# Expert weights loaded as one row and spread over the partitions by GpSimd, in place of transfers to 128 partitions

## The chip, the cores and the metric

The kernel runs on one core of one Trainium2 chip. The metric is the device time of one execution in microseconds; the time before is 358.34 us, the median of three runs (358.08 to 359.84).

## The reference

Two layers, one after the other. First attention with a learned block permutation: `sort_net` is normalised five times over rows and columns (Sinkhorn), the result mixes the 8 blocks of keys and of values of each of 4 batches x 8 heads, and softmax attention runs inside each block of 96 tokens. Its output, reshaped to 3072 tokens of 512 numbers, enters a mixture of four experts in which every token goes through every expert:

```
p = domain_probs / (domain_probs.sum(-1) + 1e-9)        # 3072 x 4
for e in range(4):
    h = maximum(x @ w1[e], 0)                            # 3072 x 1024
    out += p[:, e:e+1] * (h @ w2[e])                     # 3072 x 512
```

The change is about p, the expert weights of the tokens.

## The kernel before, in words

**Order.** The order of all instructions is written out by hand: each engine executes its own in program order, and an instruction waits by semaphore for what it reads or overwrites. Batch 0's attention runs first. From then on the experts' matmuls for 256 tokens at a time (a chunk; three chunks to a batch) alternate with pieces of the next batch's attention, which `PLANS` puts into numbered slots between the matmul groups.

**Where p is used.** In the hidden layer the tokens lie along the free axis and the features on the 128 partitions, so p of a token must stand on all partitions. The weight is put in where ReLU is applied, when a matmul result leaves PSUM: on VectorE in `chunk_first` (L821) and in `finish` (L1159), both `max(x, 0) * p`; on GpSimd in `finish2` (L1166), after a ReLU on ScalarE. So the tile `pb` (128 partitions x 4 experts x 256 tokens, float32) has to be there before the first eviction of a chunk.

**How pb is filled before.** `spread_weights` normalises p on VectorE and writes it to the scratch tensor `p_dram` (4 x 3072) in two transfers (L256, L258). `load_p` (L226 to 236) reads from it with a transfer whose source is repeated for 128 partitions; it is issued on SP, as are the attention's transposes (L413, L495), the copies of v (L405) and the stores. There is one `pb` buffer, so a load waits until the last eviction of the chunk before has read it. `load_p_one` (L238) does the same for one expert in a corner of the tile `Tt[3]`. `load_pair` (L1079) loads 256 tokens into `pb` and the next 256 into two half tiles. A chunk's load is issued by `chunk` (L845 to 851) behind the evictions of the chunk before it, with two transfers; in one chunk (batch 1, second) the second of these is held back until one product has been issued.

**GpSimd's work.** Its queue issues the loads of the expert weights `w1`, `w2` (L136 to 148, L1454 to 1479), of q, k, v (L107 to 126) and the accumulating transfers of `input_sums` (L1030). The transfers issued there use eight semaphores in turn, so the issue of one waits until the eighth before it has landed. Between them GpSimd executes `build_PI` for batch 1 (L360 to 377, four tensor_tensors), a few adds of results, and, in the last seven chunks, the multiplications of `finish2`.

**The last seven chunks** (from L1215 on). They use a scheme with seven products (Strassen-Winograd) for the first layer too. The first of them (`lead`) stands alone, the other six go in three pairs. VectorE makes the sums and differences of operands for it (`h_sums`, L779 to 791, with lines L785, L787, L789, L791 for the numbers 1 to 4; `pair_sums`, L1063; `input_sums`, L1027), all tensor_tensors with both inputs in SBUF. `load_pair` for the next pair is called in `last_second` (L1321) in the middle of the second layer of the chunk before it.

Of the kernel before, what the change touches and what calls it, by code (L numbers as in the profile page):

```python
# [2 lines left out]

# [15 lines left out]
def kernel(  # L19
# [11 lines left out]
    nc = tc.nc  # L31

    B, H, S, D = q.shape
# [4 lines left out]
    E = moe_w1.shape[0]  # L38
    FF = moe_w1.shape[2]
    P = 128  # L40
# [102 lines left out]
    def load_w2(e, parts=1):  # L143
        n = NFC // parts
        for i in range(parts):
            nc.gpsimd.dma_start(
                w2sb[e][:, ds(i * n, n)], moe_w2[e].rearrange("(fc p) d -> p fc d", p=P)[:, ds(i * n, n)]
            )
# [75 lines left out]
    pbs = {}  # L224

    def load_p(b, c, es=range(E), pb=None):  # L226
        if pb is None:
            pb = moe.tile([P, E, 2 * P], F32, name=f"pb_{b}_{c}", tag="pb", bufs=1)
        n = len(es)
        nc.sync.dma_start(  # L230
            pb[:, ds(es[0], n)],
            p_dram[ds(es[0], n), ds(b * S + 2 * c * P, 2 * P)].rearrange("(o e) x -> o e x", o=1).broadcast_to(
                [P, n, 2 * P]
            ),
        )
        return pb

    def load_p_one(b, c, e):  # L238

        pb = Tt[3].rearrange("p a f x -> p (a f x)")[:, 0:4 * P].bitcast(F32)  # L240
        nc.sync.dma_start(pb, p_dram[ds(e, 1), ds(b * S + 2 * c * P, 2 * P)].broadcast_to([P, 2 * P]))
        return pb

    def spread_weights():

        nc.vector.tensor_reduce(p_den, p_in, AX.X, ALU.add)
        yield
        nc.vector.tensor_scalar(out=p_den, in0=p_den, scalar1=1e-9, scalar2=None, op0=ALU.add)
        yield
        nc.vector.reciprocal(p_den, p_den)  # L250
        yield
        nc.vector.tensor_tensor(
            p_out.rearrange("p e t -> p t e"), p_in, p_den.broadcast_to([P, NT, E]), ALU.mult
        )
        p_rows = p_dram.rearrange("e (p t) -> p e t", t=NT)
        nc.sync.dma_start(p_rows[0:S_P], p_out[0:S_P])  # L256
        pbs[(0, 0)] = load_p(0, 0)
        nc.sync.dma_start(p_rows[S_P:P], p_out[S_P:P])  # L258
        yield

# [474 lines left out]
    def second_layer0(hf, slot):  # L735
        for t in range(R // 2):
            col = (R // 2) * hf + t
            po = psm([P, 2, 512], F32, f"ps_o_{col}")
            ps = po[:, 0, 0:Dm]
            for fc in range(NFC):  # L740
                nc.tensor.matmul(  # L741
                    ps, h0(fc)[:, ds(t * P, P)], w2sb[0][:, fc, :],
                    start=(fc == 0), stop=(fc == NFC - 1),
                )
                if fc == KH - 1:
                    slot()
            oaccs[col] = room[:, col - 2] if col > 1 else moeo.tile([P, Dm], F32, name=f"oacc_{col}", tag="oacc")
            nc.vector.tensor_scalar(
                out=oaccs[col][:], in0=ps, scalar1=p_sb[:, col], scalar2=None, op0=ALU.mult
            )  # L750
            slot()
# [82 lines left out]
    def chunk(b, c, slot, done=()):  # L834
# [8 lines left out]
            for e in es:  # L843
                h_sums(e, 2)
        nxt = (b, c + 1) if c + 1 < R // 2 else (b + 1, 0)  # L845
        first = int(nxt[0] == 0)
        pbs[nxt] = load_p(*nxt, range(first, first + 1))
        rest = lambda: load_p(*nxt, range(first + 1, E), pbs[nxt])
        late = b == c == 1
        if not late:  # L850
            rest()

        blk = lambda kh, tok: (lambda e, f: Hb[:, homes.get(e, e), kh * KH + f, ds(tok * P, P)])
        sm = lambda n: (lambda e, f: Sb[:, n, e, ds(f * P, P)])
# [26 lines left out]
        if b:  # L881
            times(bankA, blk(0, 0), "b11", es)
            slot()
            if late:
                rest()
            times(bankB, blk(1, 0), "b21", es)
            slot()
            nc.scalar.copy(p1[:], bankA)
            tt(oa1, bankB, p1[:], ALU.add)
            times(bankQ, sm(0), "t1", es)  # L890
            nc.scalar.copy(p5[:], bankQ)
            slot()
            for e in es:
                h_sums(e, 3, True)
            times(bankA, sm(1), "t2", es, False)
            nc.scalar.copy(u2[:], bankA)
            slot()
            for e in es:
                h_sums(e, 4, True)
            times(bankC, blk(1, 1), "n4", es)  # L900
            nc.scalar.copy(ob1, bankC)
            slot()
            times(bankA, blk(0, 1), "t3", es, False)
            tt(ob2, bankA, p5[:], ALU.add)
            slot()
            tt(ob1, bankA, ob1, ALU.add)
            store(1, ob)
            times(bankQ, blk(1, 0), "b22", es, False)
            tt(oa2, bankQ, u2[:], ALU.add)
            slot()  # L910
            store(0, oa)
            return
        if c:
            both = ob.rearrange("p (h d) -> p h d", h=2)
            times(bankA, blk(0, 0), "b11", es)
            slot()
            times(bankB, blk(1, 0), "b21", es)
            slot()
            tt(oa1, bankA, oa1, ALU.add)
            tt(oa1, bankB, oa1, ALU.add)  # L920
            if c == R // 2 - 1:
                h_sums(E - 3, 2)
            h_sums(E - 1, 2)
            times(bankC, blk(1, 1), "n4", es[:1], True, False)
            times(bankQ, sm(0), "t1", es)
            tt(ob2, bankQ, ob2, ALU.add)
            slot()
            for e in es:
                h_sums(e, 3)
            times(bankA, sm(1), "t2", es, False)  # L930
            tt(oa2, bankA, oa2, ALU.add)
            for e in es:
                h_sums(e, 4)
            slot()
            next(sums0)
            times(bankC, blk(1, 1), "n4", es[1:], False)
            tt(ob1, bankC, ob1, ALU.add)
            slot()
            times(bankA, sm(2), "t3", es, False)
            tt(both, bankA.rearrange("p (o d) -> p o d", o=1).broadcast_to([P, 2, DH]), both, ALU.add)  # L940
            slot()
            store(1, ob)
            next(sums0)
            times(bankQ, sm(3), "b22", es, False)
            tt(oa2, bankQ, oa2, ALU.add)
            slot()
            store(0, oa)
            return
# [6 lines left out]
        def f2():  # L955
            tt(oa1, product("p2", blk(1, 0), "b21"), oa1, ALU.add)
            slot()
# [22 lines left out]
            h_sums(e, 4)  # L980
        next(steps)
        f2()
        next(steps)
        h_sums(E - 1, 3)
        f3()
# [93 lines left out]
    def load_pair(g):  # L1079

        first, second = load_p(*divmod(g, R // 2)), []
        b, c = divmod(g + 1, R // 2)
        for n in range(2):
            t = att.tile([P, NB, 2, D], F16, name=f"pb7_{g}_{n}", tag="xsl").rearrange("p i h d -> p (i h d)")
            t = t.bitcast(F32).rearrange("p (e x) -> p e x", e=2)
            nc.sync.dma_start(
                t,
                p_dram[ds(2 * n, 2), ds(b * S + 2 * c * P, 2 * P)].rearrange("(o e) x -> o e x", o=1).broadcast_to(
                    [P, 2, 2 * P]
                ),  # L1090
            )
            second.append(t)
        pbs[g] = lambda j, e: first[:, ds(e, 1), :] if j == 0 else second[e // 2][:, ds(e % 2, 1), :]

    def last_banks(n):
# [373 lines left out]
            build_PI(nc.gpsimd, n, "k")  # L1469

    load_w2(1)
    load_w2(2)
    load_w1(3)
    def load_w2_part(e, d):
# [22 lines left out]
                f(*args)  # L1497

    second_layer0(0, next_stages)
    load_queries(1, range(2))  # L1500
    load_natural(1, "v", 0, 2, lambda: load_w2_part(3, DH))
    load_natural(1, "k", 0, 2)
    load_natural(1, "v", 1)
    load_natural(1, "k", 1)
    chunk_first(0, 0, [1, 2], 1, next_stages)
    pb_1 = load_p_one(0, 1, 1)
    h_sums(1, 4)
    for w in range(1, 5):
        h_sums(2, w)
# [3 lines left out]
    second_layer0(1, lambda: next(sums2, None))  # L1513
    sums0 = weight_sums(0, nc.vector)
    homes[1] = 0
    chunk_first(0, 1, [1], 1, next_stages, lambda e: pb_1.rearrange("p (o x) -> p o x", o=1))
    homes.clear()


    for g in range(G0 + 1):  # L1520
# [6 lines left out]
        def slot(b=b, c=c, at=at):  # L1527
            here = (c, at[0])
            for cc, n, f, *args in PLANS[b]:
                if (cc, n) == here:  # L1530
                    f(*args)
            if b:
                for cc, n, *args in PLAN_A:
                    if (cc, n) == here:
                        input_sums(*args)
                if here == (1, 12):
                    token_sums(G0, slice(0, 3))
                if here == (2, 0):
                    token_sums(G0, slice(3, 4))
            at[0] += 1  # L1540
# [6 lines left out]
    for g in range(G0 + 1, GN, 2):  # L1547
        last_second(g, last_first(g))
        last_second(g + 1, upper=True)
# [1 line left out]
_INS = ['q', 'k', 'v', 'sort_net', 'moe_domain_probs', 'moe_w1', 'moe_w2']  # L1551
_OUTS = [((3072, 512), 'float32')]
# [25 lines left out]
```

## Time and profile before

| what | us |
| --- | --- |
| median of 3 runs | 358.34 |
| the profiled execution, its own time | 358.21 |
| its span, first to last instruction | 356.3 |
| TensorE (PE) busy | 350.4 (98%) |
| VectorE (DVE) busy | 277.5 (78%) |
| ScalarE (ACT) busy | 170.1 (48%) |
| GpSimd (POOL) busy | 137.6 (39%) |
| transfers of `pb` and of the half tiles to 128 partitions | 20, of 128 to 512 KB each, landing 2.9 to 10.4 us after issue |
| the one transfer of `load_p_one` | 128 KB, landing after 12.6 |

The granted TensorE clock is full in every slice. The busy time of an engine says little by itself; the view of waits gives, for each engine, whom it waited for and how long, and the timeline gives its instructions in order with start, duration and the idle time before them. SPq and POOLq rows are the issues of transfers; a transfer lands later than its issue ends.

### The profile page before, as it was taken

The page shows a single profiled execution, that of the slowest core. Times are in us where ns is not written, and L with a number is a line of the kernel's source. Part 1 is how long each engine was busy: PE and PEld are TensorE (multiplying, and loading weights), DVE is VectorE, ACT ScalarE, POOL GpSimd, SP SyncE. Part 2 cuts the span into 40 slices and gives each one's busy share as a digit, 9 for nine tenths or more (in the row PEclk, how much of TensorE's full clock was granted, in tenths as well). Part 3 has the DMA queues.
Part 4 walks back from the last instruction along what each step waited for, and adds up shares of the span by engine and source line. Part 5 has one row for each costly group of instructions (what it writes and reads, how often), then busy time and mean ns, then how long its engine had stood idle before and what let it go on. Part 6 is the DMA issues. An engine that isn't in the chain of part 4 may idle for free.

```text
span 356.3 us, 9511 instructions
## 1 busy us (share of the span) xinstructions
PE 350.4 (98%) x3948; PEld 305.5 (86%) x3948; DVE 277.5 (78%) x555; ACT 170.1 (48%) x302; POOL 137.6 (39%) x154
## 2 busy tenths in 40 slices
PE   8899999999999999999999999999999999999996
PEld 8686857888888888988899888888888888888886
DVE  5766787779798687778879988896678886588963
ACT  2653330452425445368847259830288611598301
POOL 8766112466022420000626318840068800188400
PEclk9999999999999999999999999999999999999999
DMA  8999999999999999743995410005200014100021
GB/s 104 203 205 230 212 209 194 207 195 167 195 180 166 195 116 203 138 88 44 180 205 91 107 74 0 2 1 136 78 26 3 2 37 141 62 0 2 0 75 46
DMA packets 74762, 40.26 MB, mean 113 GB/s; under 512 B 41568, under 2 KB 70496, under 8 KB 74720
## 3 DMA queue, kind: packets, MB, share of 16 engines
q0 software_dynamic: 38720, 19.93, 43.2%
q1 hardware_dynamic: 35856, 19.67, 27.2%
q8 instruction: 31, 0.51, 0.6%
q14 instruction: 11, 0.09, 0.1%
q10 hardware_dynamic: 144, 0.07, 0.1%
HBM read 41.88 MB, written 6.34 MB: 135 GB/s over the span
## 4 chain that ended last, share of the span: by engine, by line
PE 95%; DVE 3%; issue 0%; DMA 0%; ACT 0%; DVEq 0%
PE ps_h L815 18%; PE ps_Q L1296 18%; PE ps_p L799 12%; PE ps_X L1153 10%; PE ps_Z L1153 7%; PE ps_Q L1153 7%; PE ps_Z L1296 6%; PE ps_h L704 3%; PE ps_o L741 3%; PE ps_p L860 3%; PE ps_a L479 2%; PE ps_s L444 2%; PE ps_k L425 1%; PE ps_v L391 1%; PE ps_mv L521 1%; PE ps_a L593 0%
## 5 line engine op out<-in xcount | busy, mean ns | idle before, releaser
L815 PE MATMUL ps_h<-xT,w 128*128 128x256 f16 x576 | 67.5, 273 | 0.0
L815 PEld LDWEIGHTS <-w 128*128 128x128 f16 x576 | 55.2, 98 | 7.3
L821 DVE SCALAR_TENSOR_TENSOR Hb<-ps_h,pb 128x1024 f16<-128x1024 f32 x34 | 41.5, 1223 | 17.8 <-PE ps_h L815 17.6
L1153 PEld LDWEIGHTS <-w 128*128 128x128 f16 x480 | 43.6, 98 | 4.7
L1166 POOL TENSOR_TENSOR arena<-tmp,pb 128x512 f16<-128x512 f32 x12 | 15.2, 1276 | 65.7 <-PE ps_Z L1153 49.8
L1296 PEld LDWEIGHTS <-Hb 128*128 128x128 f16 x320 | 31.1, 98 | 3.5
L1165 ACT ACTIVATE tmp<-tmp 128x512 f32<-128x512 f32 x46 | 29.0, 632 | 3.9 <-DVE tmp L1203 3.9
L1296 PEld LDWEIGHTS <-Sb 128*128 128x128 f16 x304 | 28.2, 98 | 3.0
L1153 PEld LDWEIGHTS <-arena 128*128 128x128 f16 x312 | 27.7, 98 | 2.8
L451 ACT ACTIVATE ET<-ps_s 96x768 f16<-96x768 f32 x24 | 18.1, 802 | 25.2 <-PE ps_s L444 25.0
L434 ACT CAST kT<-ps_k 64x384 f16<-64x384 f32 x48 | 22.7, 473 | 13.3 <-PE ps_k L425 12.3
L126 POOL DMA_DIRECT2D arena<-in_q_dram x24 | 19.9, 842 | 20.8 <-DMA q_ring<-arena 17.7
L1153 PE MATMUL ps_X<-ET,arena 128*128 128x256 f16 x168 | 25.2, 272 | 0.0
L1296 PE MATMUL ps_Q<-w,Hb 128*128 128x256 f16 x192 | 24.6, 273 | 0.0
L799 PEld LDWEIGHTS <-Hb 128*128 128x128 f16 x232 | 21.9, 98 | 3.0
L1159 DVE SCALAR_TENSOR_TENSOR Hb<-ps_X,pb 128x512 f16<-128x512 f32 x27 | 18.7, 692 | 7.0 <-PE ps_X L1153 7.0
L1173 ACT COPY ps_X<-ps_Z 128x512 f32<-128x512 f32 x27 | 15.4, 571 | 17.8 <-PE ps_Z L1153 17.8
L1153 PE MATMUL ps_Z<-xT,w 128*128 128x256 f16 (+1 forms) x176 | 22.5, 258 | 0.0
L785 DVE TENSOR_TENSOR Sb<-Hb 128x512 f16<-128x512 f16 x33 | 20.6, 646 | 0.0
L1180 ACT COPY tmp<-ps_X 128x512 f32<-128x512 f32 x26 | 15.2, 586 | 9.2 <-PE ps_X L1153 6.6
L1159 DVE SCALAR_TENSOR_TENSOR Hb<-ps_Z,pb 128x512 f16<-128x512 f32 x27 | 18.4, 683 | 1.3 <-PE ps_Z L1153 1.3
L1203 DVE TENSOR_TENSOR tmp<-ps_Q,tmp 128x512 f32<-128x512 f32 x26 | 17.7, 683 | 0.8 <-PE ps_Q L1153 0.8
(270 smaller groups left out, 744.3 us busy)
## 6 DMA issues: line engine op xcount, KB each, us to landing
w<-in_moe_w_dram POOLq DMA_DIRECT2D x4, 1024.0 KB, 27.2
w<-in_moe_w_dram POOLq DMA_DIRECT2D x6, 512.0 KB, 19.7
arena<-in_k_dram POOLq DMA_DIRECT2D x7, 384.0 KB, 7.6
arena<-in_v_dram POOLq DMA_DIRECT2D x7, 384.0 KB, 8.1
vs<-arena SPq DMA_DIRECT2D x36, 66.0 KB, 5.3
arena<-in_q_dram POOLq DMA_DIRECT2D x24, 96.0 KB, 7.5
out_dram<-ob SPq DMA_DIRECT2D x9, 256.0 KB, 2.0
pb<-p_dram SPq DMA_DIRECT2D x4, 512.0 KB, 5.8
```

The lines of the kernel that those rows point to most:

```text
L126: nc.gpsimd.dma_start(t[:, h // 2, :, h % 2, :], q[b, h].rearrange("(t p) d -> p t d", p=P))
L434: nc.scalar.copy(kT[ds(D * hh, D), r], pk[ds(D * r, D), hh].rearrange("p a (i c) -> p a i c", c=CP),)
L451: nc.scalar.activation(ETs[2 * (pr % 2) + hh][:, 0:S].rearrange("c (a x) -> c a x", a=2), pss[hh][0:BLK, :, 0:HS], AF.Exp, bias=0.0, scale ...
L785: tt(sm[0], blk(0, 1), blk(1, 1), ALU.add)
L799: nc.tensor.matmul(ps, lhs(e, f), Ts[e][rhs][:, f, :], start=(first and e == es[0] and f == 0), stop=(done and e == es[-1] and f == KH - 1 ...
L815: nc.tensor.matmul(ps[:, f, :], w1sb[e][:, kc, ds((4 * g + f) * P, P)], xT[:, kc, ds(2 * c * P, 2 * P)], start=(kc == 0), stop=(kc == NKC ...
L821: nc.vector.scalar_tensor_tensor(out=Hb[:, homes.get(e, e), ds(4 * g, 4), :], in0=ps[:], scalar=0.0, op0=ALU.max, in1=weights(e).broadcast ...
L1153: nc.tensor.matmul(dst[:, ds(f * cols, cols)], a[lhs][:, k, ds((f0 + f) * P, P)], t[rhs][:, k, :], start=(first and f == 0 and k == 0), st ...
L1159: nc.vector.scalar_tensor_tensor(out=home(i, j), in0=src.rearrange("p (f x) -> p f x", f=m), scalar=0.0, op0=ALU.max, in1=weight(j).broadc ...
L1165: nc.scalar.activation(src, src, AF.Relu, bias=0.0, scale=1.0)
L1203: tt(t12, Q, u2, ALU.add)
L1296: nc.tensor.matmul(ps, lhs(e, f), Ts[e][rhs][:, f, part], start=(first and e == 0 and f == 0), stop=(e == E - 1 and f == KH - 1), skip_gro ...
```

## The change

Each transfer to 128 partitions becomes a transfer to one partition (`load_rows`) and, at a place of its own further on in the program, a partition broadcast on GpSimd in place (`spread`): it reads the row in partition 0 and writes all 128 partitions. The two transfers of a chunk become one, of all its experts, and the one that was held back goes with it. The broadcast is an instruction of another GpSimd library, so a library is loaded once (between the issue of `w2` of experts 1 and 2), and the standard one again at the end. In the first chunk of all, expert 0's weights are no longer loaded; in the next one, expert 1's, which `load_p_one` brings. `load_p_one` is called before the loads of batch 1's q, k and v in place of behind the matmuls of the first chunk.

```
     def load_p(b, c, es=range(E), pb=None):
...
+        load_rows(pb[:, ds(es[0], len(es))], b, c, es)
+        return pb
+
+    def load_rows(dst, b, c, es):
         nc.sync.dma_start(
-            pb[:, ds(es[0], n)],
-            p_dram[...].rearrange("(o e) x -> o e x", o=1).broadcast_to([P, n, 2 * P]),
+            dst[0:1], p_dram[ds(es[0], len(es)), ds(b * S + 2 * c * P, 2 * P)].rearrange("(o e) x -> o e x", o=1)
         )
+
+    def spread(dst):
+        nc.gpsimd.partition_broadcast(dst, dst[0:1])
...
-        pbs[(0, 0)] = load_p(0, 0)
+        pbs[(0, 0)] = load_p(0, 0, range(1, E))
...
-        first = int(nxt[0] == 0)
-        pbs[nxt] = load_p(*nxt, range(first, first + 1))
-        rest = lambda: load_p(*nxt, range(first + 1, E), pbs[nxt])
-        late = b == c == 1
-        if not late:
-            rest()
+        first = 2 if nxt == (0, 1) else int(nxt[0] == 0)
+        pbs[nxt] = load_p(*nxt, range(first, E))
+        weights = pbs[nxt][:, first:E]
...
             times(bankA, blk(0, 0), "b11", es)          # chunk, batch 1
             slot()
-            if late:
-                rest()
+            spread(weights)
...
             times(bankB, blk(1, 0), "b21", es)          # chunk, batch 0, c > 0
             slot()
+            spread(weights)
...
         f2()                                            # chunk (0, 0)
+        spread(weights)
...
+            load_rows(t, b, c, range(2 * n, 2 * n + 2)) # load_pair
             second.append(t)
+        for t in (first, *second):
+            spread(t)
...
     load_w2(1)
+    nc.gpsimd.load_library(library_config.all_libraries[10])
+    spread(pbs[(0, 0)][:, 1:E])
     load_w2(2)
     load_w1(3)
...
     second_layer0(0, next_stages)
+    pb_1 = load_p_one(0, 1, 1)
     load_queries(1, range(2))
...
     chunk_first(0, 0, [1, 2], 1, next_stages)
-    pb_1 = load_p_one(0, 1, 1)
...
+    nc.gpsimd.load_library(library_config.standard)
```

More of the change, by code (lines that the diff above doesn't have):

```diff
@@ L5 @@
 import concourse.tile as tile
-from concourse import mybir
+from concourse import library_config, mybir
 from concourse.bass import ds
@@ L228, in load_p @@
             pb = moe.tile([P, E, 2 * P], F32, name=f"pb_{b}_{c}", tag="pb", bufs=1)
-        n = len(es)
+        load_rows(pb[:, ds(es[0], len(es))], b, c, es)
+        return pb
+    def load_rows(dst, b, c, es):
         nc.sync.dma_start(
-            pb[:, ds(es[0], n)],
-            p_dram[ds(es[0], n), ds(b * S + 2 * c * P, 2 * P)].rearrange("(o e) x -> o e x", o=1).broadcast_to(
-                [P, n, 2 * P]
-            ),
-        )
-        return pb
+            dst[0:1], p_dram[ds(es[0], len(es)), ds(b * S + 2 * c * P, 2 * P)].rearrange("(o e) x -> o e x", o=1)
+        )
+    def spread(dst):
+        nc.gpsimd.partition_broadcast(dst, dst[0:1])
     def load_p_one(b, c, e):
         pb = Tt[3].rearrange("p a f x -> p (a f x)")[:, 0:4 * P].bitcast(F32)
-        nc.sync.dma_start(pb, p_dram[ds(e, 1), ds(b * S + 2 * c * P, 2 * P)].broadcast_to([P, 2 * P]))
+        pb = pb.rearrange("p (o x) -> p o x", o=1)
+        load_rows(pb, b, c, [e])
+        spread(pb)
         return pb
@@ L1085, in load_pair @@
             t = t.bitcast(F32).rearrange("p (e x) -> p e x", e=2)
[L1086 to L1091, printed above, removed]
+            load_rows(t, b, c, range(2 * n, 2 * n + 2))
             second.append(t)
+        for t in (first, *second):
+            spread(t)
         pbs[g] = lambda j, e: first[:, ds(e, 1), :] if j == 0 else second[e // 2][:, ds(e % 2, 1), :]
@@ L1515 @@
     homes[1] = 0
-    chunk_first(0, 1, [1], 1, next_stages, lambda e: pb_1.rearrange("p (o x) -> p o x", o=1))
+    chunk_first(0, 1, [1], 1, next_stages, lambda e: pb_1)
     homes.clear()
```

## Prediction

> **What bounds the kernel.** I read the busy line of the page first, then the waits of TensorE, then the timelines of single engines where the change touches them.
>
> ```profile
> PE 350.4 (98%) x3948; PEld 305.5 (86%) x3948; DVE 277.5 (78%) x555; ACT 170.1 (48%) x302; POOL 137.6 (39%) x154
> ```
> ```profile
> PE ps_R L342 <- DVE sn L330: 1.2, 1, 1.2
> PE ps_w L276 <- DVE Hb L157: 1.1, 1, 1.1
> ```
>
> The two lines are the whole answer of the view of PE's waits (engine, tile and line, the releaser: total, times, longest). PE waits 2.3 us, both before 12 us, and then never again until its last matmul at about 353.4. The granted clock is full in all slices. So no wait on `pb` exists that could go away, and 512 KB less per chunk on the DMA engines shortens nothing: the change can only hide or add a stall. I therefore look for places where PE has little cover, and count everything against the profiled execution: 358.21 us, of which 356.3 are the span and 1.9 lie around it; the median of the runs shown, 358.34, is 0.1 above. Half a per cent is 1.8 us, and is about what a measurement of this kernel can tell from no change.
>
> The orders of PE, VectorE and ScalarE are the same in both kernels. On SP, 21 transfers to 128 partitions (20 and the one into `Tt[3]`) become 16 to one partition. GpSimd (POOL) has 18 instructions more: 16 broadcasts and two library loads.
>
> **Part 1: the library and the first broadcast.** The timeline of POOL's and SP's queues at that place (start, duration, line, what):
>
> ```profile
> 21.71 1.76 POOL L146 DMA_DIRECT2D w<-in_moe_w_dram  x2 [0.38 <-DMA w<-in_moe_w_dram]
> 23.50 0.75 POOL L139 DMA_DIRECT2D w<-in_moe_w_dram  x1
> 25.51 0.37 SPq L230 DMA_DIRECT2D pb<-p_dram  x1
> 26.10 0.89 POOL L1475 DMA_DIRECT2D w<-in_moe_w_dram  x1 [1.86 <-DMA w<-in_moe_w_dram]
> 27.00 1.06 POOL L372 TENSOR_TENSOR arena<-maskv,Rs 128x512 f16<-128x512 f16 x1
> ```
>
> The load of the library comes at 22.6, between the two issues of the first row. Its row of `p` is requested at 25.5 as before, and the broadcast waits for both. VectorE needs `pb` at 38.79 (L821), when the first matmul group of `chunk_first` ends; the group that reuses its PSUM buffer starts at 41.16, and the eviction takes 1.23, so PE is covered until the broadcast ends at 39.9. Behind it POOL has the loads of `w2` of expert 2, `w1` of 3, half of `w2` of 3, and the four `build_PI`. The transfers queued earlier hide these: `w2` of expert 1, issued at 21.71, lands 25.1 us later, at 46.8, and about 1 MB takes some 5 us of the 205 GB/s there, so the next one has to be in the queue by about 40. `build_PI` moves from 27 to 31 us to about 35 to 40, and is first read at 63.67 (L391).
>
> No row shows a library load or a broadcast. For the load the rows of the same congested stretch are: 1 us for a 16 KB block of code (the instruction queue: 31 packets, 0.51 MB, 0.6% of 16 engines' span) and 12.2 us for the slowest small transfer (L258, 36 KB). From 22.6 that ends between 23.6 and 34.8, and I take 10 us, towards the transfer, since it has to pass the same DMA engines. The row of 3 KB lies between 1.5 us (the 8 KB load of L77) and 10.4 (the whole 512 KB it replaces): 27 to 35.9. With 1.2 us for the broadcast the end lies at 28 to 37, ahead of 39.9: **0 us**. If the load took longer than 16 us, each further one would be PE's. [...] The second load, at the end, begins when POOL has finished, at 333.8; even 12.2 us end before 353: 0 us.
>
> **Part 2: the price of a broadcast.** It has one input and one output. The nearest rows are the COPY of 128x128 (L194, 0.29 us) and the adds L193 and L1166, 0.22 us at 16 elements and 1.27 at 512 (two inputs). A fixed 0.2 and 0.6 ns per element (COPY's 0.07 over 112 elements) is the lower end, 2.5 ns per element (L1166 whole) the upper. I take 0.2 us and 1.1 ns, towards COPY: 1.3 us for 1024 elements, 0.8 for 512, so 2.9 for the three of a pair (1.8 to 5.1).
>
> **Part 3: POOL's queue.** The row loads land at least as early as the transfers did, 1.5 to 8.6 us after the same SP places, and every broadcast ends before its first eviction. The one behind which most is queued is that of chunk (0, 2): POOL used to issue v and k of batch 2 at 79.84 and 80.57 and q from 81.30, but the row is requested at 85.22 only. With 2.5 to 4.5 us to land and 1.0 for the broadcast they move to about 90, q's first part to about 92. q lands up to 13.2 us after issue there, at 105, for the transpose that SP issued at 104.54, and PE uses its result at 114.23 (L444), 3.6 us behind the transpose's usual landing. Price 0. The first chunk's broadcast delays q by some 2 us at 65, with 3 us of cover (transposes at 76.82, their use at 86.15). The half that was held back at 172.26 now comes at 165.9 and delays one accumulating transfer by 1.3 us, which still lands some 5 us before its use. In all: **0 us**, up to 2.
>
> **Part 4: VectorE beside the broadcasts.** VectorE's sums read two operands from SBUF, and the profile shows what happens when GpSimd reads SBUF meanwhile:
>
> ```profile
> 196.41 1.28 POOL L1166 TENSOR_TENSOR Hb<-tmp7x,pb 128x512 f16<-128x512 f32 x1
> 196.69 1.28 DVE L785 TENSOR_TENSOR Sb<-Hb 128x512 f16<-128x512 f16 x1
> 197.64 1.45 POOL L1166 TENSOR_TENSOR Hb<-tmp7x,pb 128x512 f16<-128x512 f32 x1
> 197.89 1.48 DVE L785 TENSOR_TENSOR Sb<-Hb 128x512 f16<-128x512 f16 x1
> ```
>
> The add of L785 takes 0.42 alone (its median). Here each ends 0.28 us after the POOL instruction that had started before it: it waited for it to end. Two adds took 2.69 instead of 0.75, so of 2.68 us of POOL VectorE lost 1.94, about 0.7. [...]
>
> So I ask where VectorE's sums have less cover than 0.7 of the broadcasts beside them. At most sites it is over 1 us. In pairs two and three the rows are requested at 244.2 and 293.2; VectorE's sums of `pair_sums` end 2.9 us before PE reads them (251.98 against 254.87). The one place without cover is the load for the first pair, in the `lead` chunk:
>
> ```profile
> 200.30 1.42 DVE L787 TENSOR_TENSOR Sb<-Sb,Hb 128x512 f16<-128x512 f16 x4
> 201.64 1.42 DVE L791 TENSOR_TENSOR Hb<-Hb,Sb 128x512 f16<-128x512 f16 x4
> 202.98 1.43 DVE L789 TENSOR_TENSOR Hb<-Hb 128x512 f16<-128x512 f16 x4
> 204.92 0.42 DVE L1075 TENSOR_TENSOR kT<-xT 128x512 f16<-128x512 f16 x1
> ```
> ```profile
> 201.12 1.91 PE L1296 MATMUL ps_Q<-T,Sb 128*128 128x256 f16 x16
> 202.87 1.04 PE L1296 MATMUL ps_Q<-w,Hb 128*128 128x256 f16 x8
> 203.74 1.91 PE L1296 MATMUL ps_Q<-T,Hb 128*128 128x256 f16 x16
> 205.92 0.60 PE L1153 MATMUL ps_Q<-kT,Sb 128*128 128x256 f16 x4
> ```
>
> VectorE runs without a gap. The first sum of L789 ends at 203.39 and PE reads it at 203.74: cover 0.35 us. The row of `pb` is requested at 199.12 and lands 1.5 to 2.9 us later (L77; the fastest `pb` transfer), so the three broadcasts run from about 201.1 to 204, beside just these sums. They take 0.7 x 2.9 = 2.0 us from VectorE; less 0.35, **PE stalls 1.7 us** at the product of L789's results. The sums behind it are late by 2.0 and needed 1.7 later, so they add nothing; the next stage has 0.8 us gaps on VectorE.
>
> Sum: 358.2 + 0 + 0 + 1.7 = **359.9 us** (359.1 to 361.4 with 1.8 to 5.1 us of broadcasts: 0.7 x 1.8 - 0.35 = 0.9, 0.7 x 5.1 - 0.35 = 3.2).
>
> **Rivals.**
> *No blocking, 358.2, so no slower than before.* [...] For it: PE has cover everywhere else. Against: each POOL read next to a two-input sum in the profile blocked it. It decides if VectorE's loss in the `lead` chunk stays below 0.35 us.
> *The library comes late, 366.* The load waits for outstanding GpSimd transfers, or crawls behind the backlog (25.1 us for `w2` of expert 1). Past 39.9 us PE waits for `pb`; with 24 us it ends at 46.6, the broadcast at 47.8: 7.9 us. For it: 12 KB took 5.5 us there and 36 KB 12.2. Against: 16 KB of code cost 1 us.
> *Broadcasts at the rate of a two-input multiplication, or dearer, 363.* 3.2 us at `lead`; 1.2 in chunk (0, 2), where 1.8 us are lost against 0.55 of cover at 110.24; 0.3 in each of the later pairs: 5.0.
> *Faster, below 356.4.* It would need PE's idle time at the ends, 2.3 and some 2.8 us, which nothing here touches.
>
> **Chances.** Forecast 0.36, no blocking 0.30, late library 0.20, dear broadcasts 0.12, faster 0.02. 360.0 parts same from slower; of the forecast's 0.36 I put 0.20 above it. Slower 0.20 + 0.20 + 0.12 = 0.52, same 0.16 + 0.30 = 0.46, faster 0.02. The range, 358.0 to 367.0, leaves out the far end of a late library and what lies below. The likeliest case's own range is 359.1 to 361.4.
>
> **What would show it.** PE's waits should get one new line of 1 to 3 us, on a VectorE sum near 203; L787, L789 or L791 should show durations of 1 us or more in the `lead` chunk. A broadcast of 1024 elements should take about 1.3 us and start near 201, 246 and 295. POOL's first broadcast should end by 37. A wait of PE on the eviction L821 at 41 means a late library; a wait at 110 dear broadcasts; no new wait of PE no blocking.

## The result and the profile after

The changed kernel takes 361.3 us (median of 6 runs, 360.69 to 362.04) against 358.5 (6 runs, 358.08 to 359.84): a ratio of 1.0077, 95% interval [1.0056, 1.0098], 2.8 us more. The forecast was 359.9, the range 358.0 to 367.0: slower, as forecast, by more than the forecast had. The ratios here and below leave out an execution that is more than 1.5% above the fastest of its kernel, which concerns two executions of e9 alone. The profiled execution of the changed kernel takes 362.04 us, its span is 360.3.

The page of the kernel after, busy times and the group of broadcasts on `pb` (count, then busy time and mean ns, then idle time before them):

```profile
PE 351.7 (98%) x3948; PEld 305.8 (85%) x3948; DVE 285.4 (79%) x555; ACT 169.9 (47%) x302; POOL 153.4 (43%) x170
...
L238 POOL PARTITION_BROADCAST pb<-pb x15 | 16.8, 1177 | 62.2 <-DMA pb<-p_dram 47.4
```

GpSimd is busy 15.8 us longer; the 16 broadcasts are 17.4 us (these 15, and 0.55 for the one on `T`), and its other work overlaps or falls a little shorter. VectorE is 7.9 us longer busy with the same 555 instructions: it executes nothing new, so some of its instructions became slower. The view of PE's waits says where this reached PE. The kernel before had two rows here. In the code after, what stood from L276 to L821 stands 4 lines higher in number, later lines between 2 higher and 1 lower:

```profile
PE ps_w L280 <- DVE Hb L157: 1.1, 1, 1.1
PE ps_R L346 <- DVE sn L334: 1.0, 1, 1.0
PE ps_p L803 <- DVE room L938: 0.6, 2, 0.5
...
PE ps_Q L1295 <- DVE Hb L793: 0.4, 1, 0.4
PE ps_Q L1295 <- DVE Hb L795: 0.4, 2, 0.2
...
PE ps_s L448 <- DVE xsl L465: 0.2, 1, 0.2
PE ps_Q L1295 <- DVE Sb L791: 0.2, 1, 0.2
```

New are waits on VectorE in two places: on the sums before `ps_Q` (L791, L793, L795), which is the `lead` chunk, and on L938 and L465, in earlier chunks.

Setting the k-th matmul of this execution against the k-th of the profile before tells what each place costs, since all 3948 keep their order. The lag grows to 0.76 us by 19 us, ahead of the first changed instruction of GpSimd (kernels without a broadcast show early lags of 0.2 to 0.5 as well, so I count it to the scatter between executions). Then it grows in four steps only: 0.3 at 90.9, 0.5 at 114.6, 0.4 at 175.7 and 1.7 between 202.4 and 203.7 (times of the kernel before). From there to the end it stays at 3.7. The four steps are 2.9 us, against 2.8 between the medians. This holds for the profiled execution, the longest of the six; e3 and e9 show that the steps are not the same in all.

The last step is the forecast one. The timelines of VectorE, PE and GpSimd in the `lead` chunk of the kernel after:

```profile
202.37 2.38 DVE L791 TENSOR_TENSOR Sb<-Sb,Hb 128x512 f16<-128x512 f16 x4
204.68 2.35 DVE L795 TENSOR_TENSOR Hb<-Hb,Sb 128x512 f16<-128x512 f16 x4
206.95 1.42 DVE L793 TENSOR_TENSOR Hb<-Hb 128x512 f16<-128x512 f16 x4
```
```profile
204.81 0.61 PE L1295 MATMUL ps_Q<-T,Sb 128*128 128x256 f16 x4 [0.19 <-DVE Sb L791]
205.61 0.61 PE L1295 MATMUL ps_Q<-w,Hb 128*128 128x256 f16 x4 [0.19 <-DVE Hb L795]
206.41 0.61 PE L1295 MATMUL ps_Q<-w,Hb 128*128 128x256 f16 x4 [0.19 <-DVE Hb L795]
207.42 1.92 PE L1295 MATMUL ps_Q<-T,Hb 128*128 128x256 f16 x16 [0.40 <-DVE Hb L793]
```
```profile
203.26 2.95 POOL L238 PARTITION_BROADCAST pb<-pb  x3 [2.10 <-DVE Sb L791]
```

The two groups of four sums that lie beside the broadcasts (203.26 to 206.21) take 2.38 and 2.35 us in place of 1.42, the group behind them 1.42 as before. One at a time, the three sums that start during a broadcast take 1.38, 0.88 and 0.88 us in place of 0.41: each ends just after one broadcast does (1.35, 0.93 and 0.94 us), so one sum gets through for each. PE, which ran without a gap here, now waits four times, 0.97 us as the profile counts it; with the slower spacing of the groups of four in between it loses 1.7.

The three earlier steps, each first the broadcast, then the sum beside it, then PE's wait; this is the timeline of the kernel after by engine, at chunks (0, 2), (1, 0) and (1, 2):

```profile
90.10 1.07 POOL L238 PARTITION_BROADCAST pb<-pb  x1 [11.13 <-DMA pb<-p_dram]
...
90.18 1.40 DVE L774 TENSOR_TENSOR T<-w 128x1024 f16<-128x1024 f16 x1
...
91.97 1.25 PE L803 MATMUL ps_p<-w,Sb 128*128 128x256 f16 x10 [0.17 <-DVE room L938]
...
113.70 1.42 POOL L238 PARTITION_BROADCAST pb<-pb  x1 [9.51 <-DVE Sb L795]
...
113.20 2.05 DVE L795 TENSOR_TENSOR Sb<-Hb,Sb 128x512 f16<-128x512 f16 x3
...
116.25 1.47 PE L803 MATMUL ps_p<-w,Sb 128*128 128x256 f16 x12 [0.46 <-DVE room L938]
...
172.45 1.89 POOL L238 PARTITION_BROADCAST pb<-pb  x1
...
172.97 1.69 DVE L1029 TENSOR_TENSOR w<-arena,w 128x1024 f16<-128x1024 f16 x1
...
177.73 0.51 PE L448 MATMUL ps_s<-q_ring,kT 64*128 64x96 f16 x15 [0.21 <-DVE xsl L465]
```

Before, the same VectorE work took 0.69, 1.09 and 0.68 us:

```profile
89.39 0.69 DVE L770 TENSOR_TENSOR T<-w 128x1024 f16<-128x1024 f16 x1
...
112.09 1.09 DVE L791 TENSOR_TENSOR Sb<-Hb,Sb 128x512 f16<-128x512 f16 x3
...
171.38 0.68 DVE L1027 TENSOR_TENSOR w<-arena,w 128x1024 f16<-128x1024 f16 x1
```

It lost 0.71, 0.96 and 1.01 us, and PE was late by 0.3, 0.5 and 0.4. So the cover there was some 0.4, 0.5 and 0.6 us. The profile before has the first two as they stand: L937 frees the PSUM buffer at 90.41 and 114.12, and PE starts to write it at 90.85 and 114.61.

### The profile page after: what moved, and what is told of

It reads as the page before. It is cut to its first block, busy times and chain, and to the rows that moved or that the text cites. A ratio compares the mean times of both kernels' runs of the same rounds, so it can differ in the third digit from the quotient of the medians.

```text
span 360.3 us, 9517 instructions
## 1 busy us (share of the span) xinstructions
PE 351.7 (98%) x3948; PEld 305.8 (85%) x3948; DVE 285.4 (79%) x555; ACT 169.9 (47%) x302; POOL 153.4 (43%) x170
## 4 chain that ended last, share of the span: by engine, by line
PE 86%; DVE 9%; DMA 1%; issue 1%; SPq 1%; ACT 1%; DVEq 0%
PE ps_h L819 18%; PE ps_Q L1295 15%; PE ps_X L1152 10%; PE ps_p L803 7%; PE ps_Z L1152 7%; PE ps_Q L1152 7%; PE ps_Z L1295 6%; PE ps_h L708 3%; PE ps_o L745 3%; PE ps_p L861 3%; PE ps_s L448 1%; PE ps_a L483 1%; PE ps_v L395 1%; DVE Sb L789 1%; DMA vs<-arena 1%; PE ps_k L429 1%
## 5 line engine op out<-in xcount | busy, mean ns | idle before, releaser
L825 DVE SCALAR_TENSOR_TENSOR Hb<-ps_h,pb 128x1024 f16<-128x1024 f32 x34 | 41.5, 1223 | 16.3 <-PE ps_h L819 14.4
L238 POOL PARTITION_BROADCAST pb<-pb x15 | 16.8, 1177 | 62.2 <-DMA pb<-p_dram 47.4
```

Of the source, the lines that this page charges most:

```text
L238: nc.gpsimd.partition_broadcast(dst, dst[0:1])
L825: nc.vector.scalar_tensor_tensor(out=Hb[:, homes.get(e, e), ds(4 * g, 4), :], in0=ps[:], scalar=0.0, op0=ALU.max, in1=weights(e).broadcast ...
```

## The experiments

**Theory.** The whole cost is that of VectorE's sums, with two inputs in SBUF, held up by GpSimd's broadcasts at four places without enough cover. **Rivals.** The library loads cost something; the writes of 128 partitions, not the reads, do the blocking; the rows, their requests or the order of GpSimd's queue cost something of their own.

**e1: the first pair by transfers to 128 partitions, no broadcasts there.**

```diff
-            load_rows(t, b, c, range(2 * n, 2 * n + 2))
+            (load_wide if wide else load_rows)(t, b, c, range(2 * n, 2 * n + 2))
...
-        for t in (first, *second):
-            spread(t)
+        if not wide:
+            for t in (first, *second):
+                spread(t)
```

> The changed kernel, but the first pair's weights (requested in the lead chunk) come by transfers to 128 partitions again, without the three broadcasts there. Blocking theory (VectorE's sums with two SBUF inputs wait for each broadcast): the four waits of PE on L791, L793 and L795 near 203 to 207 go, PE's way from the product of sm(0) to the product of L793's results is 4.36 us as in the kernel before, in place of 6.02, and the time falls by 1.7 us, to about 359.6 (361.3 less 1.7). Rival, queue order (rows that land late, GpSimd's own queue): no broadcast was waited for there by an eviction, so the time stays at 361.3. Rival, library (the load and the code of the other library cost the 2.8 us): stays at 361.3.

Measured: 359.71 us, ratio 1.0041 [1.0029, 1.0054] to the kernel before. PE's waits of e1 (its lines are 7 higher) keep the earlier places and nothing in the `lead` chunk:

```profile
PE ps_p L810 <- DVE room L945: 0.6, 2, 0.5
PE ps_s L455 <- DVE xsl L472: 0.2, 1, 0.2
```

The matmuls lag by steps of 0.3, 0.5 and 0.4 at the same three places and by none at 202. So the `lead` chunk is worth 1.0077 - 1.0041, 0.36% or 1.3 us, by the times, and 1.7 us by the profiles; the intervals of the two ratios allow for that difference.

**e2: the three broadcasts of the first pair twice.**

```diff
-        for t in (first, *second):
+        for t in (first, *second) * (2 if g == G0 + 1 else 1):
             spread(t)
```

> The changed kernel with the three broadcasts of the first pair issued twice, the second time over the same data (the result is the same). Blocking theory: 2.9 us more of GpSimd reading SBUF beside VectorE's sums, of which VectorE loses about 0.7, so 2.0 us more: about 363.3, with longer L793, L1029 or L1077 (the sums after those that are hit now). Queue rival and library rival: the evictions that need the weights come 5 us later, so 361.3.

Measured: 364.14 us, 1.0156 [1.0132, 1.0179]; 0.8 above the expected 363.3. The direction holds; the excess is shown by the stretches of its profile (PE, PEld, DVE, ACT, POOL busy; the granted clock of PE; DMA share, GB/s) and by PE's waits:

```profile
207.00:209.00 2.00, 0.43 (x4) 0.40 (x5) 2.00 (x4) 0.00 (x0) 1.37 (x2) 1.00 0.00 0
209.00:211.00 2.00, 2.00 (x15) 1.55 (x14) 1.97 (x6) 0.00 (x0) 0.00 (x0) 0.71 0.00 0
211.00:213.00 2.00, 2.00 (x12) 1.43 (x10) 1.85 (x5) 0.57 (x1) 0.00 (x0) 0.50 0.00 0
```
```profile
PE ps_Q L1295 <- DVE Hb L793: 2.3, 1, 2.3
```

PE waits 2.3 us in one piece, and behind the wait its granted clock falls to one half: 12 matmuls in 2 us where the kernel after has 21. Over the executions it is the same: the three with a mean granted clock of 0.995 took 364.14 to 364.96 us, the two at 0.999 took 362.26 and 363.13. The stall costs a second time in the former. e10 tests that.

**e3: the first pair's broadcasts held behind the last sum** by a one-element addition on GpSimd that reads that sum's result.

```diff
+        if after is not None:
+            nc.gpsimd.tensor_tensor(tick, after[:, 0:1], after[:, 1:2], ALU.add)
+        for t in last["spreads"]:
+            spread(t)
```

> The changed kernel with the same row transfers and the same three broadcasts of the first pair, but these wait until VectorE has made the last of the pair's sums (a one-element add on GpSimd that reads it stands ahead of them). Blocking theory: no two-input sum that PE is about to read runs beside them, so PE's waits near 203 to 207 go; the broadcast of 1024 elements ends about when the first eviction needs it, so 0 to 0.5 us may come back: 359.6 to 360.1. Queue rival: later broadcasts can only cost, 361.3 or more.

Measured: 359.04 us, 1.0021 [1.001, 1.0032], better than expected. The broadcasts start at 207.19 and the step in the `lead` chunk is gone, so it was their place beside the sums and not their presence. The steps at chunks (0, 2) and (1, 0) are missing too, though nothing was changed there. GpSimd and VectorE at these two places in e3 (its lines are 1 higher):

```profile
89.79 1.23 POOL L239 PARTITION_BROADCAST pb<-pb  x1 [11.57 <-DMA pb<-p_dram]
...
89.43 0.68 DVE L775 TENSOR_TENSOR T<-w 128x1024 f16<-128x1024 f16 x1
90.03 0.42 DVE L939 TENSOR_TENSOR room<-ps_p,room 128x256 f32<-128x256 f32 x1
...
113.34 1.63 POOL L239 PARTITION_BROADCAST pb<-pb  x1 [8.84 <-DMA pb<-p_dram]
...
113.12 0.68 DVE L775 TENSOR_TENSOR T<-w 128x1024 f16<-128x1024 f16 x1
113.72 0.42 DVE L939 TENSOR_TENSOR room<-ps_p,room 128x256 f32<-128x256 f32 x1
```

Here the sum had started before the broadcast and keeps its 0.68 us, and the next VectorE instruction, which takes one input from PSUM (`ps_p`), runs through the broadcast in its usual 0.42. In the kernel after, L774 started 0.08 us behind the broadcast and took 1.40. Against VectorE's work the broadcasts came 0.4 and 0.7 us later in e3. Which of VectorE's instructions a broadcast meets hangs on some tenths of a microsecond, so these two steps come in one execution and not in another.

**e4: the kernel before with the two library loads alone.**

```diff
     load_w2(1)
+    nc.gpsimd.load_library(library_config.all_libraries[10])
     load_w2(2)
...
+    nc.gpsimd.load_library(library_config.standard)
```

> The kernel before with the two library loads and nothing else of the change. Blocking theory: 358.5 as before, since no broadcast runs, and GpSimd's tensor_tensors take 1.27 us as before. Library rival: 1 us or more above 358.5. It also tells whether the 0.8 us by which PE is late at 28 us in the profile of the changed kernel has to do with the load.

Measured: 358.44 us, 1.0007 [0.9998, 1.0016]: the library costs nothing that is measured. GpSimd's queue in e4 shows its length, since nothing else stands between these issues:

```profile
22.06 0.88 POOL L146 DMA_DIRECT2D w<-in_moe_w_dram  x1 [0.52 <-DMA w<-in_moe_w_dram]
28.55 1.07 POOL L146 DMA_DIRECT2D w<-in_moe_w_dram  x1 [5.60 <-issue]
```

5.60 us pass in which GpSimd waits for nothing that the profile shows.

**e5: all four places by transfers to 128 partitions**, but each of the three chunks' loads as one transfer in place of two: 384 KB for (0, 2), 512 KB for (1, 0) and (1, 2).

```diff
-        pbs[nxt] = load_p(*nxt, range(first, E))
+        far = nxt in ((0, 2), (1, 0), (1, 2))
+        pbs[nxt] = load_p(*nxt, range(first, E), wide=far)
```

> The changed kernel with transfers to 128 partitions again at the four places where PE was found late: the chunks (0, 2), (1, 0), (1, 2) and the first pair. Ten broadcasts of the 16 stay, and both library loads. Blocking theory: 358.4 to 358.7, no line of PE's waits after 30 us. Rival (each broadcast costs something everywhere, or the queue and the library do): ten sixteenths of the 2.8 us stay, about 360.

Measured: 359.93 us, 1.0047 [1.003, 1.0065]: a miss, made by my edit. VectorE and PE of e5 at chunk (0, 2):

```profile
98.44 2.36 DVE L832 SCALAR_TENSOR_TENSOR Hb<-ps_h,pb 128x1024 f16<-128x1024 f32 x2 [4.03 <-DMA pb<-p_dram]
...
99.72 3.65 PE L826 MATMUL ps_h<-xT,w 128*128 128x256 f16 x32 [2.45 <-DVE Hb L832]
```

The one transfer of 384 KB was requested at 87.1 and in use at 98.4, 11.3 us later; the kernel before sends 128 KB and 256 KB, each of which landed after 7.7. PE waits 2.45 us for the weights. So the two transfers of the kernel before are not to be joined here as long as they go to 128 partitions.

**e6 and e7: the kernel before with work on GpSimd beside the sums of the `lead` chunk**, which nothing uses: five memsets of 128x512 f32 (e6, only writes) or two subtractions of the same size (e7, two inputs from SBUF each). A one-element addition holds them until L787's first sums are done.

```diff
+            nc.gpsimd.tensor_tensor(tick, Sb[:, 1, 0, 0:1], Sb[:, 1, 0, 1:2], ALU.add)
+            for _ in range(5):
+                nc.gpsimd.memset(idle, 0.0)
```

> The kernel before, with five GpSimd memsets of 128x512 float32 over a tile whose content is no longer needed (about 2.5 us, estimated from 0.28 us for 128x128; none reads SBUF), started in the lead chunk when VectorE's first L787 is done. [...]

> As the run with the memsets, but with two GpSimd tensor_tensors of 128x512 float32 there (2 x 1.27 us; they read SBUF). Blocking theory: VectorE loses 0.7 x 2.54 = 1.8 us, PE 1.4 us: 359.6. [...]

Measured: e6 358.35 us, 1.0002 [0.9993, 1.0011]; e7 359.75 us, 1.0048 [1.0033, 1.0064]. The timelines, first e6, then e7 (lines are 1 higher than before):

```profile
200.71 1.41 DVE L788 TENSOR_TENSOR Sb<-Sb,Hb 128x512 f16<-128x512 f16 x4
...
201.44 2.85 POOL L1339 MEMSET q_ring<- 128x512 f32 x5
...
202.04 1.41 DVE L792 TENSOR_TENSOR Hb<-Hb,Sb 128x512 f16<-128x512 f16 x4
```
```profile
200.37 2.26 DVE L788 TENSOR_TENSOR Sb<-Sb,Hb 128x512 f16<-128x512 f16 x4
...
201.13 2.40 POOL L1339 TENSOR_TENSOR q_ring<-q_ring 128x512 f32<-128x512 f32 x2
...
202.55 2.26 DVE L792 TENSOR_TENSOR Hb<-Hb,Sb 128x512 f16<-128x512 f16 x4
```

2.85 us of writes leave the sums at their length (1.41 us for four); 2.40 us of reads take 1.7 us from them (0.84 and 0.85), 0.7 of their own time. Had the writes held the sums up as reads do, 0.7 of 2.85 us less 0.35 of cover, some 1.6 us, would have been lost by my estimate. The three broadcasts of the kernel after, which read one partition each, took 1.9 us from the sums in 2.95 us: they behave like the reads of e7 and not like the writes of e6.

**e8: all 16 broadcasts kept, those at the four places held behind sums** in the manner of e3.

```diff
+        def spread_behind(x):
+            nc.gpsimd.tensor_tensor(tick, x[:, 0:1], x[:, 1:2], ALU.add)
+            spread(weights)
```

> The changed kernel with all 16 broadcasts, of which four wait for sums as in the run with the first pair: in (0, 2) and (1, 0) behind the last L795, in (1, 2) behind the last L795 too, and in the first pair behind the last of its sums. Blocking theory: PE's waits at about 92, 116, 177 and 203 to 207 go, so 358.3 to 359.0. Rivals: 361.3 or more, since all broadcasts, rows and loads are the same and come later.

Measured: 359.17 us, 1.0023 [1.0014, 1.0033], just above the expected 358.3 to 359.0. Of the 2.8 us, 0.8 are left, of which its profile shows one step of 0.3 near 180: the broadcasts can be placed to cost little, not to gain.

**e9: as e5, with the loads of the four places cut in two and held back exactly as in the kernel before.** Ten broadcasts stay (the text below says nine), with the library.

```diff
-        pbs[nxt] = load_p(*nxt, range(first, E), wide=far)
+        pbs[nxt] = load_p(*nxt, range(first, first + 1) if far else range(first, E), wide=far)
+        rest = lambda: load_p(*nxt, range(first + 1, E), pbs[nxt], wide=True)
+        late = b == c == 1
+        if far and not late:
+            rest()
```

> The changed kernel, with the four places where its first profile showed PE late (chunks (0, 2), (1, 0), (1, 2) and the first pair) loaded by transfers to 128 partitions exactly as in the kernel before, cut in two where that one cuts them and held back where that one holds them back. The other nine broadcasts and both library loads stay. Theory (the whole cost is VectorE's sums blocked at four places; e5 missed because its one 384 KB transfer came later than the two it stands for): 358.2 to 358.7, and no wait of PE over 0.3 us after 20 us. Rival (the remaining broadcasts, the library or the later requests cost something of their own): 359.2 or more, with the waits of PE as in e5 gone.

Measured: ratio 1.0021 [1.0004, 1.0037], 0.75 us, between the theory and the rival. The profiled execution took 358.57 us, shows no wait of PE later than 20 us and lags by 0.2 at the end, as the theory has it. Of the other eleven, nine lie between 358.12 and 360.37; two took 363.96 and 363.99, with a mean granted clock of 0.995, the value that the profiles of e2 and e10 have for one stretch at half clock, and are not in the ratio. So a part of the executions pays something that the profiled one did not. By the times, then, the four places are worth 2.0 of the 2.8 us, and 0.75 stay with the other ten broadcasts.

**e10: e7 with four subtractions in place of two.**

> The kernel before, with four additions of 128x512 f32 on GpSimd (each reads two operands from SBUF; results used by nothing) beside VectorE's sums in the lead chunk instead of the two of e7. Theory A (only the time that VectorE loses counts): two of them cost 1.5 us, so four cost about 2.4 us more of VectorE's time, 0.7 of it lost: 1.5 + 1.7 = 3.2 us, 361.4, granted clock full. Theory B (as the profile with the broadcasts doubled suggests: when PE waits over 2 us in a row or so, its granted clock falls to one half for some microseconds): 362.5 to 363.5, with a granted clock near 0.5 in a stretch behind the wait.

Measured: 362.94 us, 1.0119 [1.0103, 1.0135], theory B's. Three of the four executions, with a mean granted clock of 0.995, took 362.85 to 363.12; the fourth kept the full clock and took 361.8, near theory A's 361.4. Stretches of e10 (columns as for e2), and PE there:

```profile
203.00:205.00 2.00, 1.03 (x8) 0.44 (x6) 2.00 (x2) 0.37 (x1) 1.84 (x3) 1.00 0.86 300
205.00:207.00 2.00, 0.61 (x4) 0.31 (x4) 2.00 (x5) 0.00 (x0) 1.01 (x1) 0.85 0.06 19
207.00:209.00 2.00, 1.98 (x10) 1.43 (x11) 1.97 (x6) 0.00 (x0) 0.00 (x0) 0.50 0.00 0
209.00:211.00 2.00, 2.00 (x16) 1.63 (x15) 1.64 (x5) 0.17 (x1) 0.00 (x0) 0.79 0.00 0
```
```profile
207.02 3.28 PE L1297 MATMUL ps_Q<-T,Hb 128*128 128x256 f16 x16 [1.24 <-DVE Hb L790]
```

The 16 matmuls take 3.28 us in place of 1.92. The lag is 3.3 us where the waits end and 4.6 some microseconds later: 1.3 us are the clock's. No broadcast is needed for it.

**e11 and e12: the remainder of e9 in two halves.** e11 is e9 with all nine loads of the pairs as transfers to 128 partitions (four early broadcasts stay). e12 is the kernel before with the library loads, and with rows and broadcasts for the second and third pair alone (six).

```diff
-        wide = g == G0 + 1
+        wide = True
```
```diff
+        if g > G0 + 1:
+            for t in (first, *second):
+                nc.gpsimd.partition_broadcast(t, t[0:1])
```

> What is left of e9, split in two, since e9 came out 0.2% above the kernel before without a wait in its profile. Here the four broadcasts of the first-layer stages that e9 kept (first chunk, the single expert, chunks (0, 1) and (1, 1)) stay, with both library loads; all nine of the pairs are transfers to 128 partitions as before. If the early rows carry the remainder (rows that land behind a full queue, early, where cover is small): 359.0, ratio 1.002. If the pairs carry it: 358.4, ratio within 0.0010 of 1.

> The kernel before with both library loads, and with rows and broadcasts for the second and third pair alone (six broadcasts). The other half of e9's remainder: if the pairs carry it (six broadcasts of which some block sums of pair_sums), 359.0, ratio 1.002; if the early rows carry it, 358.4, within 0.0010 of 1. If both come out within 0.0010, the remainder of e9 is not of either half alone and stays open.

Measured: e12 358.44 us, 0.9998 [0.9987, 1.0009]: six broadcasts and the library cost nothing. e11 358.6 us, 1.002 [0.9997, 1.0044]: seven of its twelve executions lie between 358.26 and 358.63, as before, and five from 359.31 to 363.04 (this one at a granted clock of 0.995). So what is left of e9 sits with the four early rows, if anywhere, and comes only in some executions; the interval of e11 reaches to 1, and its profile, of an execution without it, shows no wait but the two that the kernel before has. What happens in the others stays open. One candidate, which no run tests: the profiles name the broadcast of the single expert, behind `build_PI` on GpSimd, as what released the first eviction (L825), and it ended only 0.2 to 0.4 us before that eviction started (39.49 against 39.66 in the kernel after).

## Why the prediction was right, and where it was short

- **Bound by PE, nothing to gain: right.** Packets move 34.1 MB in place of 40.3, and no run came out faster than the kernel before.
- **Part 1, the library at nothing: right, the duration too long.** e4 shows no cost and 5.60 us at the place of the load, where I took 10. I had leaned towards the slowest transfer, taking the load to pass the DMA engines as the blocks of the instruction queue do. That was an estimate from that row; the load itself shows in no queue: the pages of before and after both have 31 instruction packets with 0.51 MB and 11 with 0.09 MB. The first broadcast in the kernel after waited for its row, not for the library:

```profile
31.25 1.05 POOL L238 PARTITION_BROADCAST pb<-pb  x1 [8.09 <-DMA pb<-p_dram]
```

  It ended at 32.3, inside the forecast 28 to 37.
- **Part 2, the price: right.** 1024 elements took 1.30 us where no sum was in the way (up to 1.89 where one was, at chunk (1, 2)) and three broadcasts of a pair 2.89 to 2.95, against 1.3 and 2.9. With 0.55 for 256, 0.80 for 512 (e1, at 69.49) and 1.05 for 768 elements that is some 0.3 us and 1.0 ns per element.
- **Part 3, GpSimd's queue at nothing: right for PE's waits, but one row landed late.** At chunk (1, 0) it was requested at 107.07 and the broadcast started at 113.70, over 6 us later (in e3, where the profile names the row as what was waited for, 105.88 and 113.34); I had 2.5 to 4.5 to land. Transposes stand on the same queue, but that they are the reason is not shown. That laid this broadcast beside L795.
- **Part 4, the `lead` chunk: right.** Forecast: three broadcasts from 201.1, 2.0 us taken from VectorE, 1.7 us of PE. Measured: they start at 203.26, or some 201.2 when the lag of 2.0 is taken off, VectorE loses 1.9, PE 1.7 (1.3 by the times of e1). That a broadcast takes 0.7 of its own time from the sums, as the tensor_tensors of L1166 did, was my estimate: no row of the profile before shows it for a broadcast; the kernel after shows 1.9 of 2.95 us, 0.64. The shape is another: in place of one wait of 1 to 3 us PE has four of 0.19 to 0.40, and loses the rest to the slower sums in between. e1, e3 and e7 show each link: no broadcasts, no stall; broadcasts later, no stall; another reader, a stall again (1.0048); e6 that 2.85 us of writes cost nothing (1.0002).
- **The step that failed** is the sentence "At most sites it is over 1 us", by which all other places were priced at nothing. At chunks (0, 2), (1, 0) and (1, 2) the cover was 0.4 to 0.6 us against losses of 0.7 to 1.0: 0.3 + 0.5 + 0.4 = 1.2 us in the profiled execution, of the 1.4 between 359.9 and 361.3. By the times e9 leaves these three places 1.0041 - 1.0021, some 0.7 us, and as much again to what stays open there. The covers stood in the profile before; I had one like them, 0.55 us at 110.24, in the third rival's working, and set it only against a dearer broadcast. At pairs two and three the sentence held (e12). That a broadcast met a sum at (0, 2) and (1, 0) is in part chance, as e3 shows.
- **Rivals.** "No blocking" fell with the kernel after and with e7; "late library" with e4; "dear broadcasts" with the measured price, though the stage it named beside `lead`, chunk (0, 2) at 110, into which the row of (1, 0) falls, was one of those that paid, 4 us later.

## What to carry to other kernels

Here GpSimd instructions that read SBUF took 0.5 to 0.7 of their own duration from VectorE's sums with two SBUF inputs (a broadcast of one row 1.01 of 1.89 us at chunk (1, 2), two tensor_tensors 1.7 of 2.40 in e7), and where VectorE ran without a gap just ahead of TensorE, in the `lead` chunk, 1.7 of 1.9 us reached it. So write the cover down for every place at which such an instruction lands, not for the tightest alone. Put it beside VectorE work that reads PSUM (0.42 us beside a broadcast as without one, e3), or behind the sums with a small dependent instruction (ratios of 1.0021 in e3 and 1.0023 in e8, in place of 1.0077). This kernel, TensorE busy for 98% and without a wait on these transfers, gained nothing from lighter ones: 34.1 MB in place of 40.3, 361.3 us in place of 358.5.

## What the runs showed of the hardware

- At chunk (0, 2) it mattered which started first: a sum already running kept its length (0.68 us in e3), one that started 0.08 us behind a broadcast ended only after it (1.40 in the kernel after). An instruction with one input in PSUM beside a broadcast took its usual 0.42 (e3, at 90.03 and 113.72).
- In one place it went the other way: in e1 the broadcast for chunk (1, 1) started 0.14 us behind a sum and took 3.78 us in place of 1.30, while eight two-input sums that followed on each other beside it (from 141.40 on) kept their 0.41 each. Why the sums won here and lost in the `lead` chunk is not shown:

```profile
141.54 3.78 POOL L245 PARTITION_BROADCAST pb<-pb  x1 [8.92 <-DVE xsl L472]
```

- In two profiles TensorE was mostly idle for some 4 us and paid again. In e2 (busy 1.5 of 4 us from 205, longest wait 2.3) the granted clock was 0.71, 0.50 and 0.94 in the three stretches of 2 us from 209, in e10 (busy 1.6 of 4 us from 203, longest wait 1.24) 0.85, 0.50 and 0.79 in those from 205: as if it had stood at one half for about 3.4 us (an estimate: the sum of what the stretches lack, doubled); in the kernel after, with 3.4 us busy of the same 4, it stayed full. It does not always follow: in e5 PE was busy for no more (1.55 of 4 us, longest wait 2.45), and the clock stayed full in these stretches and in the 6 us behind them (32 matmuls in 3.65 us from 99.72, 32 in 3.66 from 103.70), as it did throughout in one of e10's four executions. What decides is not shown. The two stretches of e5:

```profile
96.00:98.00 2.00, 1.27 (x15) 1.06 (x13) 0.00 (x0) 1.29 (x3) 0.00 (x0) 1.00 1.97 200
98.00:100.00 2.00, 0.28 (x3) 0.25 (x3) 1.55 (x2) 1.27 (x3) 0.00 (x0) 1.00 2.33 137
```
